# Sliding-window attention and an MLP mixer on one core: q and k turned by VectorE 32x32 transposes, scores on four 32-row tiles, an instruction order from a list schedule

## The chip, the cores and the metric

The kernel runs on one core of one Trainium2 chip. A core has five engines with instruction queues of their own, each strictly in order: TensorE (PE in the profile; its weight loads are listed apart as PEld), VectorE (DVE), ScalarE (ACT), GpSimd (POOL) and SyncE (SP, which here only issues DMAs). Matrix products land in PSUM, eight banks of 128 partitions x 512 fp32; everything else works out of SBUF. The metric is the device time of one execution in microseconds, as the median of the runs shown; lower is better.

## The reference

```
q, k, v: [4, 8, 768, 64] fp32          # batch, heads, sequence, head dim
scores = (q @ k^T) / 8                 # 768 x 768 for each batch and head
keep   = (key < 4) | (0 <= query - key < 128)     # 4 sink keys, a window of 128
x      = softmax(where(keep, scores, -1e9)) @ v   # then heads side by side: [4, 768, 512]
h      = relu(x^T @ w_tok1) @ w_tok2   # over the sequence, 768 -> 256 -> 768
u      = x + h^T
out    = u + relu(u @ w_ch1) @ w_ch2   # over the channels, 512 -> 1536 -> 512
```

All inputs and the output are fp32 in HBM. The kernel rounds to bf16 on the chip and accumulates in fp32.

## The kernel before, in words

The sequence is cut into NT = 6 tiles of 128. Attention is worked in groups of GH = 4 heads, two groups to a batch (g = 0 to 7), and a group in pairs j of heads. `tiles`, `load_q`, `load_k` and `load_v` bring a group's q, k and v as fp32; q and k in rows of 1536 bytes (partition p holds the positions 6p to 6p+5), v in 256-byte rows. `cast` and `cast_v` make bf16 of them, on POOL for groups 1 to 7 (`begin`). `tr` (L193) turns q and k: six PE transposes with the identity into one PSUM tile, and one DVE copy out of it that also restores the order of positions; a small DVE copy (L202) takes the four sink keys into `kz`. `sc` (L219) makes scores with keys on the partitions: for each key tile only the 128 or 256 queries that the window can reach, two heads beside each other on two 64-row tiles of PE; groups 0 and 1 first put a -30000 mask into PSUM with an identity matmul (L213). The exponent (L225, ACT) writes `pT`; for groups 2 to 7 POOL masks it afterwards (L229, L236, L239). `sk` (L246, L248) does the sink keys of the later query tiles. `pv` (L253 to L265) multiplies by v, with a column of ones for the sum, and DVE divides into `x_b`.

The mixer of a batch: `tok1` (L285, relu on ACT L287), `tok2` (L292, with u = x + h by DVE L293), `utr` (L298, PE transposes of u, copied by ACT L299), `ch1` (L304, C1: 24 of four matmuls, relu on ACT L306) and `ch2` (L313, C2: 18 of four matmuls, the sum with u on DVE L316, then the store on SP).

The order on each engine is the order in which the program emits instructions. For batch 0 it is a list written by hand; from then on `spread` puts the attention, token mixing and turns of batch b+1 (the `order` list) at given shares of the way through C1 and C2 of batch b. A load of group g+2 is issued when group g begins; group 2's load also waits for w_ch1 (`after`). PSUM is split by purpose: `ps_sc` two tiles of two banks (scores), `ps_mx` two banks (mixer matmuls), `ps_ms` two banks (transposes, sinks, PV). The weights are loaded and cast by DMAs issued on POOL.

Of the kernel before, what the change touches and what calls it, by code (L numbers as in the profile page):

```python
# [12 lines left out]
ALU = mybir.AluOpType  # L13


@with_exitstack
def kernel(
# [13 lines left out]
    nc = tc.nc  # L31
# [12 lines left out]
    HS = S // 2  # L44
    D1 = D + 1
    scale = 1.0 / float(D) ** 0.5

    singles = ctx.enter_context(tc.tile_pool(name="singles", bufs=1))
    stage = ctx.enter_context(tc.tile_pool(name="stage", bufs=2))
    bfp = ctx.enter_context(tc.tile_pool(name="bfp", bufs=2))  # L50
    att = ctx.enter_context(tc.tile_pool(name="att", bufs=3))
    ptp = ctx.enter_context(tc.tile_pool(name="ptp", bufs=4))
    small = ctx.enter_context(tc.tile_pool(name="small", bufs=4))
    xpool = ctx.enter_context(tc.tile_pool(name="xpool", bufs=2))
    mix = ctx.enter_context(tc.tile_pool(name="mix", bufs=2))
    osb = ctx.enter_context(tc.tile_pool(name="osb", bufs=4))
# [5 lines left out]
    mask0 = singles.tile([P, 2, 2, P], BF16, name="mask0")  # L62
    mneg = singles.tile([P, 2, 2, 2, P], BF16, name="mneg")
    warm = singles.tile([P, 512], BF16, name="warm")
    ks = [[singles.tile([P, P], BF16, name=f"ks{a}{j}") for j in range(2)] for a in range(2)]
    vs_f = singles.tile([4 * GH, NG, GH, D1], FP32, name="vs_f")
    vsink = singles.tile([P, NG, GH, D1], BF16, name="vsink")

# [5 lines left out]
    SYNC = mybir.DependencyInfo(mybir.DependencyClass.Sync, mybir.DependencyReason.DATA)  # L74

    def after(dma, *others):
        for o in others:
            tc.add_manual_dep(dma.ins, o.ins.name, SYNC, reason="order of loads")
        return dma
# [4 lines left out]
    def tiles(g):  # L84
        G = Group()
        G.b, G.h0 = g // GB, GH * (g % GB)
        G.q32 = stage.tile([P, GH, NT, D], FP32, name="q32")
        G.k32 = stage.tile([P, GH, NT, D], FP32, name="k32")
        G.qb = bfp.tile([P, 2, NT, 2, D], BF16, name="qb")
        G.kb = bfp.tile([P, 2, NT, 2, D], BF16, name="kb")  # L90
        G.v32 = stage.tile([P, GH, NT, D], FP32, name="v32")
        G.va = bfp.tile([P, GH, NT, D1], BF16, name="va")
        G.qT, G.kT, G.pT = [None, None], [None, None], [None, None]
        return G


    def load_qk(eng, src, dst, G, lo, hi):
        return eng.dma_start(
            out=dst[:, lo:hi].rearrange("p h t d -> p h (t d)"),
            in_=src[G.b, G.h0 + lo:G.h0 + hi].rearrange("h (p t) d -> p h (t d)", t=NT))  # L100

    def load_q(G, lo, hi, eng=nc.sync):
        return load_qk(eng, q, G.q32, G, lo, hi)

    def load_k(G, lo, hi, eng=nc.sync):
        return load_qk(eng, k, G.k32, G, lo, hi)

    def cast(G, j, which, copy):
        src, dst = ((G.q32, G.qb), (G.k32, G.kb))[which]
        copy(dst[:, j].rearrange("p t i d -> p i t d"), src[:, 2 * j:2 * j + 2])  # L110

    def by_dve(o, i):
        nc.vector.tensor_copy(out=o, in_=i)  # L113

    def by_pool(o, i):
        nc.gpsimd.tensor_copy(out=o, in_=i)

    def by_act(o, i):
        nc.scalar.activation(o, i, AF.Copy)

    def load_v(G):
        return nc.sync.dma_start(out=G.v32.rearrange("p h t d -> p (h t) d"),
                                 in_=v[G.b, G.h0:G.h0 + GH].rearrange("h (t p) d -> p (h t) d", p=P))

    def load_sinks():
        for h in range(GH):
            nc.sync.dma_start(
                out=vs_f[4 * h:4 * h + 4, :, h, 0:D],
                in_=v.rearrange("b (a h) s d -> h s (b a) d", h=GH)[h, 0:4])

    def load_tok():
        nc.gpsimd.dma_start(out=w_tok1, in_=moe_w_tok1.rearrange("(t p) n -> p t n", p=P))
        nc.gpsimd.dma_start(out=w_tok2, in_=moe_w_tok2.rearrange("(t p) n -> p t n", p=P))

    def load_ch1(i):
        hf = DCH // 2
        return nc.gpsimd.dma_start(out=w_ch1[:, :, ts(i, hf)],
                            in_=moe_w_ch1.rearrange("(t p) n -> p t n", p=P)[:, :, ts(i, hf)])

    def load_ch2(i):  # L140
        hf = NF // 2
        nc.gpsimd.dma_start(out=w_ch2[:, ts(i, hf)],
                            in_=moe_w_ch2.rearrange("(t p) n -> p t n", p=P)[:, ts(i, hf)])

    def build_masks():

        z = mneg.rearrange("p m x c q -> p (m x) c q")
        nc.gpsimd.affine_select(
            out=z[:, :, 0], in_=z[:, :, 0], compare_op=ALU.is_ge,
            fill=-30000.0, base=0, pattern=[[0, 4], [1, P]], channel_multiplier=-1)  # L150
        nc.gpsimd.affine_select(
            out=z[:, :, 1], in_=z[:, :, 1], compare_op=ALU.is_ge,
            fill=-30000.0, base=-1, pattern=[[0, 4], [-1, P]], channel_multiplier=1)
        nc.vector.memset(mneg[0:4, 0, 0], 0.0)

    def build_mask0():
        nc.vector.memset(mask0, 1.0)
        nc.gpsimd.affine_select(
            out=mask0[:, :, 0], in_=mask0[:, :, 0], compare_op=ALU.is_ge,
            fill=0.0, base=0, pattern=[[0, 2], [1, P]], channel_multiplier=-1)  # L160
        nc.gpsimd.affine_select(
            out=mask0[:, :, 1], in_=mask0[:, :, 1], compare_op=ALU.is_ge,
            fill=0.0, base=-1, pattern=[[0, 2], [-1, P]], channel_multiplier=1)
        nc.vector.memset(mask0[0:4], 1.0)

    def build_sinks():

        one = vs_f[:, :, :, D]
        nc.gpsimd.memset(one, 1.0)
        nc.gpsimd.affine_select(  # L170
            out=one, in_=one, compare_op=ALU.is_ge, fill=0.0,
            base=0, pattern=[[0, NG], [-4, GH]], channel_multiplier=1)
        nc.gpsimd.affine_select(
            out=one, in_=one, compare_op=ALU.is_ge, fill=0.0,
            base=3, pattern=[[0, NG], [4, GH]], channel_multiplier=-1)

    def cast_sinks():
        nc.vector.tensor_copy(out=vsink[0:4 * GH], in_=vs_f)

    def cast_v(G):  # L180
        nc.gpsimd.memset(G.va[:, :, :, D:D1], 1.0)
        nc.gpsimd.tensor_copy(out=G.va[:, :, :, 0:D], in_=G.v32)


    def attention(g, G, x_b, first):
        c0 = GH * D * (g % GB)
        kz = ks[g % 2]

        def tr(j, which):
            src = G.qb if which == 0 else G.kb  # L190
            ps = ps_ms.tile([P, NT, P], BF16, name="ps_tr", tag="ms")
            for t in range(NT):
                nc.tensor.transpose(ps[:, t], src[:, j, t].rearrange("p i d -> p (i d)"), ident)  # L193
            dst = att.tile([P, S], BF16, name="qT" if which == 0 else "kT")
            (by_act if g == 0 and j == 0 and which else by_dve)(
                dst.rearrange("d (p t) -> d p t", t=NT), ps.rearrange("d t p -> d p t"))
            if which == 0:
                G.qT[j] = dst
            else:
                G.kT[j] = dst  # L200
                for i in range(2):
                    nc.vector.tensor_copy(out=kz[j][ds(64 * i, 64), ds(8 * j + 4 * i, 4)],  # L202
                                          in_=ps[ds(64 * i, 64), 0:4, 0])

        def sc(j, u):
            if u == 0:
                G.pT[j] = ptp.tile([P, 2, 12 * P], BF16, name="pT")
            ps = ps_sc.tile([P, 2, 512], FP32, name="ps_s", tag="sc")
            kts = [(kt, (2 if kt < NT - 1 else 1) * P) for kt in (2 * u, 2 * u + 1)]
            n = sum(w for _, w in kts)  # L210
            if first:
                for i in range(2):
                    nc.tensor.matmul(ps[:, i, 0:n], ident,  # L213
                                     mneg[:, min(u, 1)].rearrange("p x c q -> p (x c q)")[:, 0:n],
                                     start=True, stop=False, skip_group_check=True)
            at = 0
            for kt, w in kts:
                for i in range(2):
                    nc.tensor.matmul(  # L219
                        ps[:, i, at:at + w],  # L220
                        G.kT[j][ds(64 * i, 64), ts(kt, P)], G.qT[j][ds(64 * i, 64), ds(kt * P, w)],
                        start=not first, stop=not first or at > 0, skip_group_check=first)
# [266 lines left out]
```

## Time and profile before

| | us |
|---|---|
| median of the 2 runs | 239.63 (239.11 to 240.16) |
| span of the profiled execution (first to last instruction) | 237.1 |
| PE busy in the span | 212.1 |
| DVE, ACT, POOL busy | 100.6, 114.1, 88.9 |

The profiled execution's own time is not given apart from its span. The span is one execution; the runs lie 2.0 to 3.1 us above it, so differences are formed on the span, and 2.5 us are added to compare with the median. In a row of the table of stretches stand the stretch, its length, the busy time of PE, PEld, DVE, ACT and POOL with the count of instructions, the granted PE clock, the busy share of the DMA engines and what they moved in GB/s. In a row of a group stand line, engine, operation, output<-input, shapes and count, then total busy time, the mean of one in ns, and the idle time ahead of it with what ended it. A row of the timeline begins with start and duration in us. A matmul's listed duration includes its way through the array; what it costs the next one is the distance between starts.

### The profile page before, as it was taken

What the parts mean: (1) busy time and instruction counts of PE and PEld (TensorE: products, weight loads), DVE (VectorE), ACT (ScalarE), POOL (GpSimd) and SP (SyncE); (2) the same over time, 40 slices, a digit from 0 to 9 for tenths busy, and PEclk for the clock granted to TensorE, in tenths of its full rate; (3) what the DMA queues carried; (4) which work ended last, traced back from release to release, by engine and by line L of the source; (5) the groups of instructions that cost most, each with busy time, mean ns of one, the idle gap of its engine ahead of it and who ended that gap; (6) DMA issues with size and microseconds to landing.
All of it is one profiled execution on the core that took longest, in us unless ns stands there. A gap on an engine that the chain in (4) does not pass through costs nothing.

```text
span 237.1 us, 4195 instructions
## 1 busy us (share of the span) xinstructions
PE 212.1 (89%) x1708; PEld 119.8 (51%) x1729; DVE 100.6 (42%) x221; ACT 114.1 (48%) x195; POOL 88.9 (37%) x124
## 2 busy tenths in 40 slices
PE   6797788976999999978999999978999999999993
PEld 2334545552556544645566445635566445554441
DVE  5687663070845454707526334707526334001131
ACT  2585536759472123595772233695762133653300
POOL 3567400449989200079985000089950000000000
PEclk9999999999999999999999999999999999999999
DMA  6999999999994111893911021100001021101122
GB/s 215 303 258 144 206 189 258 283 327 248 267 328 109 72 44 44 240 205 90 304 54 44 0 91 46 44 0 3 13 34 44 14 78 44 46 3 44 44 88 88
DMA packets 40659, 29.40 MB, mean 124 GB/s; under 512 B 25664, under 2 KB 37696, under 8 KB 40640
## 3 DMA queue, kind: packets, MB, share of 16 engines
q1 hardware_dynamic: 36000, 23.89, 36.8%
q0 software_dynamic: 3680, 3.93, 10.1%
q10 hardware_dynamic: 960, 1.31, 1.6%
q8 instruction: 13, 0.21, 0.4%
q14 instruction: 6, 0.05, 0.1%
HBM read 26.77 MB, written 6.29 MB: 139 GB/s over the span
## 4 chain that ended last, share of the span: by engine, by line
PE 68%; POOL 10%; DVE 9%; ACT 6%; DMA 3%; issue 2%; ACTq 0%; POOLq 0%
PE ps_w L313 26%; PE ps_v L304 20%; DVE o L316 5%; ACT pT L225 5%; PE ps_h L285 3%; PE ps_tr L193 3%; PE ps_u L292 3%; DMA k_113<-in_k_dram 3%; PE ps_s L219 3%; POOL pT L236 2%; PE ps_ut L298 2%; PE ps_o L257 2%; PE ps_o L253 2%; DVE x_b L265 2%; POOL pT L239 2%
## 5 line engine op out<-in xcount | busy, mean ns | idle before, releaser
L304 PE MATMUL ps_v<-uT,w_ch_103 128*128 128x384 bf16 x384 | 74.3, 325 | 1.4 <-ACT uT L299 0.7
L304 PEld LDWEIGHTS <-w_ch_103 128*128 128x128 bf16 x384 | 34.7, 97 | 25.0 <-issue 6.8
L225 ACT ACTIVATE pT<-ps_s 128x1024 bf16<-128x1024 f32 (+1 forms) x48 | 43.6, 961 | 7.1 <-PE ps_s L219 6.9
L229 POOL TENSOR_TENSOR pT<-pT,mask_92 128x512 bf16<-128x512 bf16 x12 | 13.8, 1154 | 52.2 <-ACT pT L225 52.2
L316 DVE TENSOR_TENSOR o<-ps_w,u_sb 128x512 f32<-128x512 f32 x24 | 16.6, 692 | 39.5 <-PE ps_w L313 39.5
L113 DVE COPY qT<-ps_tr 128x768 bf16<-128x768 bf16 x16 | 15.3, 957 | 35.2 <-PE ps_tr L193 35.0
L299 ACT ACTIVATE uT<-ps_ut 128x512 bf16<-128x512 bf16 x24 | 14.0, 596 | 32.6 <-PE ps_ut L298 32.5
L293 DVE TENSOR_TENSOR u_sb<-ps_u,x_b 128x512 bf16<-128x512 f32 x24 | 16.4, 689 | 25.9 <-PE ps_u L292 25.9
L265 DVE TENSOR_TENSOR x_b<-ps_o,rc 128x256 bf16<-128x256 f32 x48 | 20.4, 424 | 1.7
L236 POOL TENSOR_SCALAR_AFFINE_SELECT pT<-pT 128x640 bf16<-128x640 bf16 x24 | 18.0, 752 | 5.5 <-ACT pT L225 5.5
L219 PE MATMUL ps_s<-qT,kT 64*128 64x256 bf16 x192 | 15.5, 263 | 4.6 <-ACT pT L225 3.1
L264 DVE RECIPROCAL rc<-ps_o 128x4 f32<-128x4 f32 x48 | 8.5, 178 | 25.9 <-PE ps_o L261 13.1
L313 PE MATMUL ps_w<-w_ch_104,v_581 128*128 128x512 bf16 x69 | 18.1, 379 | 0.8 <-DVE o L316 0.6
L313 PE MATMUL ps_w<-w_ch_104,v_1338 128*128 128x512 bf16 x69 | 18.1, 379 | 0.8 <-DVE o L316 0.6
L313 PE MATMUL ps_w<-w_ch_104,v_111 128*128 128x512 bf16 x67 | 17.9, 379 | 0.8 <-DVE o L316 0.3
L306 ACT ACTIVATE v_1338<-ps_v 128x384 bf16<-128x384 f32 x24 | 11.9, 506 | 12.5 <-PE ps_v L304 12.5
L306 ACT ACTIVATE v_581<-ps_v 128x384 bf16<-128x384 f32 x24 | 11.9, 506 | 12.6 <-PE ps_v L304 12.6
L257 PE MATMUL ps_o<-va,pT 128*128 128x65 bf16 x192 | 17.3, 194 | 0.2
L306 ACT ACTIVATE v_2035<-ps_v 128x384 bf16<-128x384 f32 x24 | 11.8, 491 | 11.3 <-PE ps_v L304 11.2
L257 PEld LDWEIGHTS <-pT 128*128 128x128 bf16 x192 | 14.5, 98 | 3.5 <-issue 0.4
L306 ACT ACTIVATE v_111<-ps_v 128x384 bf16<-128x384 f32 x24 | 11.8, 495 | 9.0 <-PE ps_v L304 8.8
L313 PE MATMUL ps_w<-w_ch_104,v_2035 128*128 128x512 bf16 x70 | 15.9, 379 | 0.1
(102 smaller groups left out, 280.2 us busy)
## 6 DMA issues: line engine op xcount, KB each, us to landing
out_dram<-o SPq DMA_DIRECT2D x23, 256.0 KB, 2.0
w_ch_103<-in_moe_w_ch_dram POOLq DMA_DIRECT2D x2, 768.0 KB, 9.4
w_ch_104<-in_moe_w_ch_dram POOLq DMA_DIRECT2D x2, 768.0 KB, 13.8
k_113<-in_k_dram ACTq DMA_DIRECT2D x2, 384.0 KB
q_112<-in_q_dram SPq DMA_DIRECT2D x2, 384.0 KB, 5.8
q_118<-in_q_dram SPq DMA_DIRECT2D x2, 384.0 KB, 5.5
v_116<-in_v_dram SPq DMA_DIRECT2D x1, 768.0 KB, 10.9
v_122<-in_v_dram SPq DMA_DIRECT2D x1, 768.0 KB, 7.2
```

The costliest lines, as they stand in the source:

```text
L113: nc.vector.tensor_copy(out=o, in_=i)
L219: nc.tensor.matmul(ps[:, i, at:at + w], G.kT[j][ds(64 * i, 64), ts(kt, P)], G.qT[j][ds(64 * i, 64), ds(kt * P, w)], start=not first, stop= ...
L225: nc.scalar.activation(pT[:, :, 512 * u:512 * u + n], ps[:, :, 0:n], AF.Exp, scale=scale)
L236: nc.gpsimd.affine_select(out=cur, in_=cur, compare_op=ALU.is_ge, fill=0.0, base=0, pattern=[[0, NT - 1], [1, P]], channel_multiplier=-1)
L257: nc.tensor.matmul(ps[:, h], pT[:, i, ds(256 * qt, P)], G.va[:, h, qt], start=(qt < 2 and h == 0), stop=(h == GH - 1 and qt == 0), skip_gr ...
L265: nc.vector.tensor_tensor(out=x_b[:, qt, c0:c0 + GH * D].rearrange("p (h d) -> p h d", h=GH), in0=ps[:, :, 0:D], in1=rc.to_broadcast([P, G ...
L293: nc.vector.tensor_tensor(out=u_sb[:, st], in0=ps, in1=x_b[:, st], op=ALU.add)
L299: nc.scalar.activation(uT[:, :, ts(st, P)], ps, AF.Copy)
L304: nc.tensor.matmul(ps, w_ch1[:, c, ts(ft, P)], uT[:, c, ds(half * HS, HS)], start=(c == 0), stop=(c == NC - 1))
L306: nc.scalar.activation(v1[:, ft, ds(half * HS, HS)], ps, AF.Relu)
L313: nc.tensor.matmul(ps, v1[:, ft, ts(st, P)], w_ch2[:, ft], start=(ft == 0), stop=(ft == NF - 1))
L316: nc.vector.tensor_tensor(out=o, in0=ps, in1=u_sb[:, st], op=ALU.add)
```

## The change

- q and k: no PE transposes, no PSUM. A group's q lies with head h on the partitions 32h to 32h+31, so that each 32x32 block transposed by DVE puts 32 of the 64 head dimensions of head h on those same partitions. `turn` does one half of the head dimension (db = 0, 1) of all four heads at once, with unit-stride output. Loads are issued for each head (`head_load`): 1 KB pieces for groups 0 and 1 (whose positions come out permuted, undone in the exponent's access pattern and by small PE matmuls for v), 256-byte pieces from group 2 on.
- Scores: the head dimension is summed in two steps of 32, on four 32-row tiles of PE, one for each head (two at a time in groups 0 and 1). Only group 0 masks in PSUM; group 1 is masked on DVE, groups 2 to 7 on DVE (the first block) and on POOL or DVE.
- Order: every step is an `Op` with planned durations; `order_of` simulates the engines, the PSUM slots and the DMAs, and emits the steps in the order that it finds. Attention and token mixing of batch b+1 have priority over C1 and C2 of batch b. Some steps (relus, u's transposes' copies, v's copies) go to ACT or DVE as the planner finds.
- PSUM: two score tiles of two banks as before, and four banks shared by everything else.
- Sinks come by a casting DMA on POOL; v's bf16 tiles are three fixed buffers; fp32 loads share five buffers; batch 0's token mixing is done for each group apart; w_ch1 comes in quarters.

The core of the diff:

```diff
-    ps_sc = ctx.enter_context(tc.tile_pool(name="ps_sc", bufs=2, space=bass.MemoryType.PSUM))
-    ps_mx = ctx.enter_context(tc.tile_pool(name="ps_mx", bufs=2, space=bass.MemoryType.PSUM))
-    ps_ms = ctx.enter_context(tc.tile_pool(name="ps_ms", bufs=2, space=bass.MemoryType.PSUM))
+    slots = {"sc": 2, "mx": 4}
+    stage = ctx.enter_context(tc.tile_pool(name="stage", bufs=5))
...
+def order_of(ops, slots):
...
+    def start(op, e):
+        t = free_at[e]
+        for d in op.deps:
+            t = max(t, d.end + lag(d, op, e))
+        if op.take:
...
+        if e == "PE" and op.rows != rows:
+            t += 0.095
...
+            first = min(t for t, _ in c)
+            t, o = min(((t, o) for t, o in c if t <= first + 0.2), key=lambda x: (x[1].pri, -x[1].far, x[1].seq))
...
+def act(n):
+    return (n + 205) / 1200
+def dve(n, rate=1):
+    return (n / rate + 150) / 960
...
+    def head_load(eng, G, w, src, h, lo, hi, run):
...
+        eng.dma_start(
+            out=G.raw[w][Q * h:Q * h + Q].rearrange("p (c x) -> p c x", x=run * D)[:, at:at + n],
+            in_=src[h, lo:hi].rearrange("(c i e) d -> i c (e d)", i=Q, e=run))
...
+        def turn(w, hf, db, c):
+            def emit(e):
...
+                nc.vector.transpose(G.T[w][:, db, ds(hf * HS, S // n_half)],
+                                    G.bf[w][:, hf].rearrange("p (r x j) -> p r x j", x=DB, j=Q)[:, :, db])
+            old = (prev.sc + [prev.sk]) if prev else []
+            return op(f"T{w}{g}.{hf}{db}", ("DVE", dve(nc_ / 2) - 0.06), emit, [c] + old, early)
...
+                for kt, w in nk:
+                    for db in range(DB):
+                        for h in hs:
+                            r = ds(Q * h, Q)
+                            nc.tensor.matmul(bank[h][:, at:at + w], G.T["k"][r, db, ts(kt, P)],
+                                             G.T["q"][r, db, ds(kt * P, w)],
+                                             start=not pem and db == 0, stop=db == DB - 1,
+                                             skip_group_check=True, tile_position=(Q * h, 0))
+                    at += w
...
+                r = [op(f"MK{g}.0h", ("DVE", dve(1024, 2)), head, ex + [c_maske_op if perm else c_mask_op], base + u)]
...
+                    r.append(op(f"MK{g}.{u}{x}{c}", {"DVE": dve(512, 2)} if perm else {"POOL": 0.72, "DVE": dve(512, 2) + 0.1}, lambda e, x=x, c=c: block(e, x, c),
+                                ex + [c_maske_op if perm else c_mask_op], base + u, dear={"DVE": 0.6}))
...
+            o = op(f"C1{b}.{hf}{ft}", ("PE", 0.652), emit,
+                   [t for st in range(NH * hf, NH * hf + NH) for t in M.ute[st]] + [w_ops["ch1", ft // 3]], pri, take=[p])
...
+            M.v1[hf].append(op(f"V{b}.{hf}{ft}", {"ACT": act(HS), "DVE": dve(HS)}, relu, [o] + old, pri - 5, free=[p]))
...
+            if g >= 2:
+                deps = [c1w[3]] if g < 4 else []
+                deps += groups[g - 2].cast + (groups[g - 1].cast if g >= 3 else [])
+                load_ops(g, deps, 1000 * b - 700)
+            attention(g, batches[b].x, 1000 * b + 10 * a)
+        mixer(b, 1000 * b + 50, 1000 * b + 1100)
...
+        for o in order_of(ops, slots):
+            o.emit(o.engine)
```

The dependencies between steps are for the planner alone. On the chip an instruction waits for the data and the buffers that it uses, and for what stands ahead of it in its engine's queue.

More of the change, by code (lines that the diff above doesn't have):

```diff
@@ L13, with __init__ @@
 ALU = mybir.AluOpType
+INF = float("inf")
+class Psum:
+    def __init__(self, kind, readers):
+        self.kind, self.left, self.slot, self.tile = kind, readers, None, None
+class Op:
+    n = 0
+    def __init__(self, name, engines, emit, deps=(), pri=0, rows=False, take=(), free=(), land=0.0, dear=None):
+        self.name, self.engines, self.emit = name, engines, emit
+        self.deps, self.pri, self.rows = [d for d in deps if d is not None], pri, rows
+        self.take, self.free, self.land, self.dear = take, free, land, dear or {}
+        self.far = 0.0
+        self.begin = self.end = self.engine = None
+        Op.n += 1
+        self.seq = Op.n
@@ L72, with op @@
     w_ch2 = singles.tile([P, NF, DM], BF16, name="w_ch2")
[L74 to L79, printed above, removed]
+    ops = []
+    def op(name, engines, emit, deps=(), pri=0, **kw):
+        if not isinstance(engines, dict):
+            engines = dict([engines])
+        o = Op(name, engines, emit, deps, pri, **kw)
+        ops.append(o)
+        return o
@@ L81, with heads @@
+    def heads(src, g):
+        b, h0 = g // GB, GH * (g % GB)
+        return src[b, h0:h0 + GH]
     class Group:
         pass
[L84 to L94, printed above, removed]
@@ L97, in load_qk @@
[L97 to L110, printed above, removed]
@@ L112, in by_dve @@
[L112 to L129, printed above, removed]
@@ new lines @@
+    stores = []
+    w_ops = {}
+    o_warm = op("warm", ("DVE", 0.27), c_warm, (), -200)
+    c_ident_op = op("ident", ("POOL", 0.6), c_ident, (), -200)
+    o_zero = op("zero", ("DVE", 0.5), c_zero, (), -199)
+    o_mneg = op("mneg", ("POOL", 1.4), c_mneg, [o_zero], -199)
+    o_idp = op("identp", ("DVE", 0.2), c_ident_e, [c_ident_op], -199)
+    c_mneg_op = op("mnegs", ("DVE", 0.17), c_mneg_sink, [o_mneg, o_idp], -199)
+    c_kz_op = op("kz", ("DVE", 0.3), c_kz, (), -150)
+    o_vs = op("vsink", ("DVE", 1.2), c_vsink, (), -140)
@@ new lines, with weight, emit @@
+    c_maske_op = op("meo", ("ACT", 0.8), c_me_out, [o_me], -30, free=[me_ps])
+    def weight(key, dst, src, deps, pri=-40):
+        def emit(e):
+            nc.gpsimd.dma_start(out=dst, in_=src)
+        n = 1
+        for x in dst.shape:
+            n *= x
+        w_ops[key] = op(f"W{key}", ("POOL", 0.8), emit, deps, pri, land=n * 4e-6 / BW)
+        return w_ops[key]
+    v1st = groups[0].load["v"][3]
+    weight("tok1", w_tok1, moe_w_tok1.rearrange("(t p) n -> p t n", p=P), [v1st])
+    weight("tok2", w_tok2, moe_w_tok2.rearrange("(t p) n -> p t n", p=P), [v1st])
@@ new lines, with dummy @@
+    qf = DCH // 4
+    c1w = [weight(("ch1", i), w_ch1[:, :, ts(i, qf)], moe_w_ch1.rearrange("(t p) n -> p t n", p=P)[:, :, ts(i, qf)],
+                  [v1st], [-40, 12, 14, 16][i]) for i in range(4)]
+    c2src = moe_w_ch2.rearrange("(t p) n -> p t n", p=P)
+    weight(("ch2", 0), w_ch2[:, 0:8], c2src[:, 0:8], [c1w[0]], 40)
+    weight(("ch2", 1), w_ch2[:, 8:12], c2src[:, 8:12], [c1w[0]], 41)
+    def dummy(e):
+        p = psum["mx"][0].tile([P, 512], FP32, name="ps_warm", tag="b")
+        for _ in range(14):
+            nc.tensor.matmul(p, warm[:, 0:P], warm, start=True, stop=True)
@@ L457 @@
+    for o in ops:
+        if 0 <= o.pri < 60:
+            o.pri = 0
+    with tc.manual_schedule():
+        for o in order_of(ops, slots):
+            o.emit(o.engine)
 _INS = ['q', 'k', 'v', 'n_sink', 'window', 'moe_w_tok1', 'moe_w_tok2', 'moe_w_ch1', 'moe_w_ch2']
```

780 lines of the change are left out of this document (491 added, 289 removed).

## The prediction, made before the changed kernel was run

> **What bounds the kernel now.** I read the page's first two parts, then the table of stretches cut where a batch's channel mixer takes over PE (its first L304 matmuls at 36.57, 93.97, 146.99 and 200.02 us), then PE's waits inside those stretches.
>
> ```profile
> PE 212.1 (89%) x1708; PEld 119.8 (51%) x1729; DVE 100.6 (42%) x221; ACT 114.1 (48%) x195; POOL 88.9 (37%) x124
> PE   6797788976999999978999999978999999999993
> PEclk9999999999999999999999999999999999999999
> ```
>
> ```profile
> core 0: us, PE busy (x) PEld busy (x) DVE busy (x) ACT busy (x) POOL busy (x), PEclk, DMA share, GB/s
> 36.57:93.97 57.40, 52.16 (x435) 30.37 (x441) 24.01 (x53) 29.20 (x51) 28.85 (x38) 1.00 0.78 201
> 93.97:146.99 53.02, 49.70 (x420) 29.32 (x424) 23.50 (x52) 27.24 (x49) 24.09 (x32) 1.00 0.44 120
> 146.99:200.02 53.03, 49.72 (x421) 29.31 (x425) 23.51 (x52) 27.23 (x49) 19.54 (x26) 1.00 0.08 31
> 200.02:237.10 37.08, 32.60 (x167) 16.19 (x167) 4.84 (x7) 11.98 (x25) 0.00 (x0) 1.00 0.13 50
> ```
>
> PE is the bound from 36.57 us on, at the full granted clock. In the three middle stretches, 163.5 us, PE is idle 57.40-52.16 + 53.02-49.70 + 53.03-49.72 = 11.9 us; no other engine is busy over 56%. So there a microsecond of PE work taken out is a microsecond gained, and 11.9 us is the most that better order can give. The named part of that idleness, PE's waits from 36.5 to 201:
>
> ```profile
> PE ps_tr L193 <- POOL qb L116: 4.6, 3, 1.8
> PE ps_s L219 <- ACT pT L225: 3.1, 6, 1.0
> PE ps_w L313 <- DVE o L316: 1.6, 5, 0.4
> ```
>
> All three are in-order waits: PE stands at a transpose, a score or an output matmul while mixer matmuls behind it could run. Before 36.57 it is another kernel, a chain from the first load through both head groups of batch 0, with PE idle about a fifth of the time (the last fence of the next part).
>
> **The change part by part.** *PE transposes out.* This is the surest term.
>
> ```profile
> 110.72 0.50 PE L193 MATMUL ps_tr<-ident,kb 128*128 128x128 bf16 x6
> 111.06 0.81 PE L304 MATMUL ps_v<-uT,w_ch_103 128*128 128x384 bf16 x4
> 111.81 0.61 PE L219 MATMUL ps_s<-qT,kT 64*128 64x256 bf16 x8
> 112.35 0.82 PE L304 MATMUL ps_v<-uT,w_ch_103 128*128 128x384 bf16 x4
> ...
> 114.33 0.56 PE L219 MATMUL ps_s<-qT,kT 64*128 64x256 bf16 x8
> 114.82 1.04 PE L313 MATMUL ps_w<-w_ch_104,v_581 128*128 128x512 bf16 x4
> 115.70 0.27 PE L253 MATMUL ps_o<-vsink,pk 128*128 128x260 bf16 x1
> ```
>
> From start to start six transposes hold PE for 111.06-110.72 = 0.34 us (0.335 is the mean of such pairs). Groups 2 to 7 have four each: 6 x 4 x 0.335 = **-8.0 us**, nothing hiding it. The eight of groups 0 and 1 lie in the start, where PE waits anyway: nothing.
>
> *DVE transposes in.* Four of 128x768 a group (eight of half the size in group 0) in place of four copies out of PSUM. No row shows such an instruction; the nearest are these.
>
> ```profile
> L113 DVE COPY kT<-ps_tr 128x768 bf16<-128x768 bf16 x15 | 14.3, 952 | 0.2
> L265 DVE TENSOR_TENSOR x_b<-ps_o,rc 128x256 bf16<-128x256 f32 x48 | 20.4, 424 | 1.7
> L113 DVE CAST qb<-q_112 128x768 bf16<-128x768 f32 x2 | 1.0, 522 | 0.0
> ```
>
> By length the bounds are 0.52 us (the cast) and 0.424 x 3 = 1.27 us; I take the 0.95 of the copy it replaces. DVE's load then stays as it was, 23.5 of a 53 us batch; even at 1.27 it gains only 2.6 us a batch, under PE's 47. Nothing on the path. If that cover went, SC would be late and PE with it.
>
> *Scores on four 32-row tiles.* A group keeps three episodes of scores, with 16 matmuls each, not 8: four heads beside each other, two 32-deep halves one after the other, so the same columns pass if four tiles run side by side as two do now. In the rows above eight matmuls of 256 columns take 114.82-114.33 = 0.49 us; one alone streams for 0.65/4 x 256/384 = 0.108 (111.06 to 112.35 holds 0.65 of ps_v), so eight in a row would be 0.87. The two tiles do overlap, and their weight loads cost almost nothing (0.49 against 4 x 0.108). Twice as many loads are bounded below by nothing and above by no overlap at all (a rival below); I take a tenth, 0.05 us in 18 episodes: **+1.0 us**. [...]
>
> *Masks, casts, sinks.* In groups 2 to 7 the first block's mask moves to DVE and the others become 128x512 selects on either engine; q and k are cast whole.
>
> ```profile
> L236 POOL TENSOR_SCALAR_AFFINE_SELECT pT<-pT 128x640 bf16<-128x640 bf16 x24 | 18.0, 752 | 5.5 <-ACT pT L225 5.5
> L239 POOL TENSOR_SCALAR_AFFINE_SELECT pT<-pT 128x512 bf16<-128x512 bf16 x24 | 15.3, 638 | 0.0
> L229 POOL TENSOR_TENSOR pT<-pT,mask_92 128x512 bf16<-128x512 bf16 x12 | 13.8, 1154 | 52.2 <-ACT pT L225 52.2
> ```
>
> Nine selects of 0.64 are 5.8 us of POOL a group, against 4 x (0.75+0.64) + 2 x 1.15 = 7.9. [...] The DVE waits for ACT's exponent; behind it in its queue stand x_b, u and o, for which PE's banks wait. With four shared banks that holds PE only beyond the next three matmul groups, some 2 us.
>
> *Loads.* For groups 2 to 7 q and k come in 256-byte pieces, in four DMAs of 32 partitions, as only v does now.
>
> ```profile
> 113.00:114.00 1.00, 0.95 (x10) 0.52 (x9) 0.61 (x2) 1.00 (x2) 1.00 (x2) 1.00 1.07 399
> 117.00:118.00 1.00, 1.00 (x14) 0.55 (x12) 0.85 (x3) 0.00 (x0) 1.00 (x2) 1.00 1.39 220
> 22.00:32.00 10.00, 8.43 (x117) 5.90 (x114) 6.05 (x21) 4.60 (x7) 2.81 (x5) 1.00 1.17 206
> q0 software_dynamic: 3680, 3.93, 10.1%
> 34.60 11.82 SPq L98 DMA_DIRECT2D q_568<-in_q_dram  x1
> ```
>
> At 113 q and k of the last group flow (1536-byte pieces), at 117 its v; from 22 to 32 the weights (queue q0). So 2.36 MB a group take 2.36/0.22 = 10.7 us, not 7.6; a group has 23 us. It is hidden in the batches. Five raw buffers make SP wait for casts, as it does now (its q_568 entry stands 11.82 us); behind it are stores with four buffers, a slack of several O steps. In the start the explicit wait of group 2's load for w_ch1 is gone: from about 15 us these pieces share the engines with the 3.93 MB of weights. 19 us of weights (at 206 GB/s) and 21 of groups 2 and 3 end near 55 us. The first w_ch1 quarter is issued ahead, so I count nothing, and up to 5 us if C1 starves.
>
> *The start.*
>
> ```profile
> 0.00:10.00 10.00, 6.88 (x40) 2.88 (x41) 5.93 (x14) 3.96 (x4) 3.62 (x12) 1.00 0.84 267
> 10.00:20.00 10.00, 8.67 (x88) 3.84 (x87) 8.11 (x17) 7.71 (x9) 8.00 (x11) 1.00 1.06 213
> 20.00:30.00 10.00, 7.50 (x103) 5.03 (x104) 6.91 (x21) 4.23 (x6) 4.80 (x7) 1.00 1.17 195
> 36.57 0.81 PE L304 MATMUL ps_v<-uT,w_ch_103 128*128 128x384 bf16 x4 [0.69 <-ACT uT L299]
> ```
>
> DVE is the busiest evacuator here (20.95 of 30 us) and gets more: group 1's ten mask multiplies (about 5.5 us at 0.55), half of eight v copies (2), less the k sink copies and the fp32 sink buffer. Some 28 us of DVE work from 5.4 us on again end near 33, and token mixing follows, now split by group for batch 0 so that half is done early. I take **-1.0 us**, with 5 either way.
>
> *Order and banks.*
>
> ```profile
> L225 ACT ACTIVATE pT<-ps_s 128x1024 bf16<-128x1024 f32 x32 | 32.3, 1029 | 6.3 <-PE ps_s L219 6.3
> L264 DVE RECIPROCAL rc<-ps_o 128x4 f32<-128x4 f32 x48 | 8.5, 178 | 25.9 <-PE ps_o L261 13.1 <-PE ps_o L257 12.3
> L293 DVE TENSOR_TENSOR u_sb<-ps_u,x_b 128x512 bf16<-128x512 f32 x24 | 16.4, 689 | 25.9 <-PE ps_u L292 25.9
> 233.16 0.69 DVE L316 TENSOR_TENSOR o<-ps_w,u_sb 128x512 f32<-128x512 f32 x1 [1.90 <-PE ps_w L313]
> ```
>
> The planner's times agree with this trace where I can compare them: exponents 1.02 against 1.03, x_b 0.60 against 0.178+0.424, mixer 0.652 against 0.65, u and o 0.69 against 0.69. It puts attention of the next batch ahead of C1 and C2 and fills with those. Of the 11.9 us I take **-8.0**: the three named waits are 9.3 us, and I leave a little for lateness; bounds 0 and 11.9. Late next are the exponents (ACT 27 us a batch, most in one half). At the end 24 C1 of 0.65 and 18 C2 of 0.865 need 31.2 us, and the stretch from 200.02 to the last o (233.16) takes 33.1; four banks for two: **-1.0**, bounds 0 and 1.9.
>
> Sum: 237.1 - 8.0 + 1.0 - 1.0 - 8.0 - 1.0 = 220.1 us of span. The median of the runs is 239.63, 2.5 above the span; so 222.6, said as 222.5.
>
> **The rivals.** *The list gives nothing back.* Other waits replace the three: 237.1-8.0+1.0 = 230.1, 232.6 us, 228 to 237 with the start's bounds. For it: every list here is static, and a load that lands late holds a whole queue. Against it: the agreeing durations, and PE as the only full engine.
>
> *Everything falls into place:* all 11.9, start -5, end -1.9, scores 0: 210.3, so 212.8 and below 215 when most of it comes.
>
> *Four tiles don't overlap,* the change not doing what it says. A group then streams 40 x 0.108 + 8 x 0.055 = 4.8 us of scores, not 1.5: +19.7 in six groups, 219.1+19.7 = 238.8, or 241.3 us. The overlap of two tiles speaks against it.
>
> *Slower: attention first in PE's queue convoys.* SC stands ahead of C1; if turns or exponents are later than planned, PE stands at SC with ready mixer work behind it, and DVE, waiting for PV, delays the next turns. This is what the start looks like: from 10 to 30 us PE is idle 3.83 of 20, 19%. PE's 151.6-8.0+1.0 = 144.6 us at that share take 178.5, not 163.5: 252.1 of span, 254.6 us. It is slower than no change from an idle share of 14% (163.5+4.8 = 168.3). Now the share is 7%, and DVE and ACT at half load speak against it.
>
> **How the numbers follow.** A measurement here can tell about 2% from no change (234.8 to 244.4 us). Chances: forecast (215 to 229) 0.57; nothing back 0.18, a third of it above 234.8; all in place 0.08; no overlap 0.06; convoy 0.11, a little of it inside 2%. Faster 0.57+0.08+0.12 = 0.77; same 0.06+0.06+0.01 = 0.13; slower 0.10. The range 212 to 237 holds the first two and most of the third, 0.8 in all; the cases beyond 237 are left out.
>
> **What would show it.** Right: no L193 left; a batch's stretch near 47 to 48 us; score episodes of 0.5 to 0.6; first ps_v matmul at 33 to 38 us; DVE transposes near 0.95. Wrong: PE waiting over 2 us a batch for SC's inputs, DVE over 70% in a batch, loads at under 100 GB/s, or w_ch1 late.

## The result and the profile after

The changed kernel takes 225.38 us (224.84 and 225.93) against 239.63, a ratio of 0.942 with an interval of 0.933 to 0.951: faster by 14 us, where 17 were forecast (222.5, range 212 to 237). The profiled execution took 225.93 us with a span of 223.9.

The page of the changed kernel, busy time by engine, PE's slices and the granted clock:

```profile
PE 206.2 (92%) x1760; PEld 115.9 (52%) x1780; DVE 127.4 (57%) x271; ACT 107.5 (48%) x187; POOL 70.2 (31%) x89
PE   7298497999999999999999899999999999999994
PEclk9955569999999999999999999999999999999999
```

Two things are to be seen. From the ninth slice on PE is full, with an 8 or 9 in every slice but the last. And the start, the first eight slices of 5.6 us, has kept its gaps, with the granted clock near one half in three of them.

The join between the two parts is the first matmul of the channel mixer, ps_v: 36.57 us before. The changed kernel's view of the ps_v line (L645; minimum, median and longest duration in ns, then first and last start), its last row on DVE, and the stretch between:

```profile
L645 PE MATMUL ps_v<-uT,w_ch x384: 322/326/337, 47.6 to 210.0; 128*128 128x384 bf16 x192
```
```profile
220.71 0.42 DVE L677 TENSOR_TENSOR o<-ps_w,u_sb 128x256 f32<-128x256 f32 x1 [0.89 <-PE ps_w L667]
```
```profile
47.62:220.71 173.09, 170.35 (x1436) 97.13 (x1451) 93.25 (x188) 86.69 (x151) 52.33 (x54) 1.00 0.65 116
```

The same stretch of the kernel before, from its first ps_v to the start of its last o (233.16):

```profile
36.57:233.16 196.59, 184.17 (x1438) 105.19 (x1455) 75.17 (x164) 95.64 (x171) 72.48 (x96) 1.00 0.39 107
```

The start is 47.62-36.57 = 11.05 us longer, the rest 196.59-173.09 = 23.5 us shorter, and what follows the last o's start 0.75 (3.94 to 3.19): together -13.2, the difference of the spans. PE's listed idle time in the long stretch fell from 12.42 us to 2.74. The three waits that the prediction named are gone; the longest that are left of PE's waits there, in the changed kernel:

```profile
PE ps_v L645 <- DVE x_b L559: 0.6, 1, 0.6
PE ps_o L535 <- DVE x_b L559: 0.3, 1, 0.3
PE ps_o L535 <- ACT v L205: 0.3, 1, 0.3
```

### The profile page after: what moved, and what is told of

It is laid out like the page before. It is cut to its first block, busy times and chain, and to the rows that moved or that the text cites. A ratio compares the mean times of both kernels' runs of the same rounds, so it can differ in the third digit from the quotient of the medians.

```text
span 223.9 us, 4412 instructions
## 1 busy us (share of the span) xinstructions
PE 206.2 (92%) x1760; PEld 115.9 (52%) x1780; DVE 127.4 (57%) x271; ACT 107.5 (48%) x187; POOL 70.2 (31%) x89
## 4 chain that ended last, share of the span: by engine, by line
PE 75%; DMA 10%; DVE 7%; ACT 4%; SPq 1%; issue 1%; DVEq 0%
PE ps_w L667 27%; PE ps_v L645 26%; DMA raw_k<-in_k_dram 7%; PE ps_u L607 5%; PE ps_h L583 5%; PE ps_s L437 4%; DMA raw_v<-in_v_dram 3%; PE ps_ut L618 3%; DVE pT L477 2%; PE ps_o L538 2%; PE ps_o L543 2%; PE ps_o L535 2%; DVE x_b L559 2%; ACT pT L456 1%; SPq L304 1%
## 5 line engine op out<-in xcount | busy, mean ns | idle before, releaser
L645 PE MATMUL ps_v<-uT,w_ch 128*128 128x384 bf16 x384 | 69.0, 326 | 0.8 <-DVE x_b L559 0.6
L667 PE MATMUL ps_w<-w_ch,v 128*128 128x512 bf16 (+1 forms) x288 | 65.2, 370 | 0.8 <-issue 0.2
L205 ACT ACTIVATE v<-ps_v 128x384 bf16<-128x384 f32 x86 | 42.0, 493 | 43.2 <-PE ps_v L645 32.1
L645 PEld LDWEIGHTS <-w_ch 128*128 128x128 bf16 x384 | 35.8, 98 | 24.8 <-DVE x_b L559 1.7
L677 DVE TENSOR_TENSOR o<-ps_w,u_sb 128x512 f32<-128x512 f32 (+1 forms) x25 | 16.7, 666 | 52.0 <-PE ps_w L667 52.0
L667 PEld LDWEIGHTS <-v 128*128 128x128 bf16 x300 | 28.6, 98 | 30.2 <-issue 0.4
L456 ACT ACTIVATE pT<-ps_s 128x1024 bf16<-128x1024 f32 (+1 forms) x36 | 32.4, 950 | 20.2 <-PE ps_s L437 17.7
L212 POOL TENSOR_SCALAR_AFFINE_SELECT pT<-pT 128x512 bf16<-128x512 bf16 x21 | 15.9, 765 | 35.4 <-ACT pT L456 14.9
L437 PE MATMUL ps_s<-qT,kT 32*128 32x256 bf16 (+1 forms) x384 | 20.0, 281 | 2.6 <-DVE kT L363 1.9
L200 POOL CAST kb<-raw_k 128x1536 bf16<-128x1536 f32 x7 | 10.4, 1491 | 26.8 <-DMA raw_k<-in_k_dram 26.8
L613 DVE TENSOR_TENSOR u_sb<-ps_u,x_b 128x512 bf16<-128x512 f32 (+1 forms) x30 | 15.6, 573 | 4.2 <-PE ps_u L607 4.2
L538 PE MATMUL ps_o<-va,pT 128*128 128x65 bf16 x192 | 16.8, 199 | 0.1
L543 PE MATMUL ps_o<-va,pT 128*128 128x65 bf16 x160 | 15.6, 198 | 0.0
```

The source lines that it names most:

```text
L200: "POOL": lambda o, i: nc.gpsimd.tensor_copy(out=o, in_=i),
L205: nc.scalar.activation(o, i, AF.Relu)
L437: nc.tensor.matmul(bank[h][:, at:at + w], G.T["k"][r, db, ts(kt, P)], G.T["q"][r, db, ds(kt * P, w)], start=not pem and db == 0, stop=db = ...
L456: nc.scalar.activation(o, i, AF.Exp, scale=scale)
L538: nc.tensor.matmul(ps[:, h], G.pT[qt // 2][:, h, ds(256 * (qt % 2), P)], G.va[:, h, qt], start=(qt < 2 and h == 0), stop=(h == GH - 1 and ...
L543: nc.tensor.matmul(ps[:, h], G.pT[kt // 2][:, h, ds(256 * (kt % 2) + P, P)], G.va[:, h, kt], start=False, stop=(h == GH - 1), skip_group_c ...
```

## The experiments

**The changed kernel again**, beside others on one chip.

> The changed kernel again, as the base of the runs beside it. All theories: 224.8 to 225.9 us, first C1 matmul (ps_v) near 47.6 us, granted clock at half from about 11 to 32 us.

225.12 us (224.73 to 226.11), ratio 0.942 (0.938 to 0.947). The experiments are compared with this run and with the kernel before on their own chip (238.7 to 239.2 us everywhere). Its first ps_v starts at 47.1. In its stretch table the loads of groups 0 and 1 stand at 207 GB/s with a DMA share of 1.16, and its last v, group 1's, is cast at 25.65:

```profile
10.00:18.00 8.00, 7.05 (x48) 2.48 (x48) 5.74 (x10) 5.31 (x7) 1.63 (x3) 0.67 1.16 207
```
```profile
25.65 0.96 DVE L199 CAST vb<-raw_v 128x1536 bf16<-128x1536 f32 x1 [2.75 <-DMA raw_v<-in_v_dram]
```

**Loads of groups 0 and 1 across all 128 partitions**, with the same 1 KB pieces:

```diff
+        if run > 1:
+            for c in range(h, n, GH):
+                eng.dma_start(
+                    out=G.raw[w].rearrange("p (c x) -> p c x", x=run * D)[:, at + c],
+                    in_=src[:, lo + P * c:lo + P * c + P].rearrange("h (i e) d -> h i (e d)", e=run))
+            return
```

> Groups 0 and 1 are loaded with the same 1 KB pieces, but each DMA takes one chunk of 128 positions of all four heads and so writes 128 partitions, not 32; the order on all engines is the same. Theory: the start is late because it waits for loads, and these are slow because a DMA writes only 32 partitions. Then the first 20 us move near 390 GB/s, not 205, the second cast of v comes at 16 to 18 us, not 26.6, the first ps_v matmul at 37 to 40, and the time is 216 to 218 us. Rival, small pieces: 1 KB pieces are as slow as 256-byte ones wherever they go; the rate stays near 205 and the time within 1 us of 225. Rival, the clock: PE's half clock from 11 to 32 us makes the start late; the loads may get faster but the time falls by 3 us at most.

274.32 us, ratio 1.148 (1.142 to 1.154): a miss as a cure, but the clearest test of the start. The stretch, the cast of group 1's v, and the first ps_v:

```profile
10.00:18.00 8.00, 1.79 (x6) 0.53 (x6) 2.44 (x5) 2.13 (x2) 0.87 (x3) 0.50 0.28 91
```
```profile
73.32 0.96 DVE L199 CAST vb<-raw_v 128x1536 bf16<-128x1536 f32 x1 [22.89 <-DMA raw_v<-in_v_dram]
95.08 10.56 PE L651 MATMUL ps_v<-uT,w_ch 128*128 128x384 bf16 x64
```

The DMA share fell to 0.28, what four to five engines of sixteen would give if they were always busy. The source's outermost dimension is now the four heads; whether that is the cause was not shown. Two things follow. Over its share of busy time an engine moves 91/(16 x 0.28) = 20 GB/s with 1 KB pieces here, against 207/(16 x 1.16) = 11 in the changed kernel, an estimate from these two rows, so the size of the pieces is not what slows the changed kernel's loads. And group 1's v came 73.32-25.65 = 47.7 us later, the first ps_v 95.08-47.1 = 48.0, the end 49.2: with the list unchanged, the start follows the landing of these loads, one for one.

**A warm clock**: more opening matmuls.

```diff
-        for _ in range(14):
+        for _ in range(30):
```

> 30 warm-up matmuls in place of 14, so that PE is busy until the first scores. Theory, the start waits for loads: the granted clock may stay at 1.0, but the first ps_v matmul moves by less than 1 us and the time is 224 to 226 us. Rival, the half clock is the cause of the late start: first ps_v at 37 to 42 us, 215 to 220 us.

225.98 us, ratio 0.945 (0.939 to 0.951), no change. The clock now is whole through the stretch that had 0.67, and the loads, at 206 GB/s for 207, do not care:

```profile
10.00:18.00 8.00, 6.54 (x61) 2.73 (x60) 5.42 (x10) 7.05 (x11) 1.55 (x3) 1.00 1.16 206
```

The first ps_v stands at 47.2. So as far as the clock was held, to about 22 us, its being halved is not what makes the start late. What the half clock costs between 22 and 32 us was not separated. Nor do the last v and the first ps_v move quite together here: that v was cast at 26.37, 0.7 us later than in the changed kernel, and the first ps_v came 0.1 later, so up to 0.6 us may be the clock's.

**Two row tiles at a time** in groups 2 to 7.

```diff
-            if g < 2:
+            if True:
```

> Groups 2 to 7 make scores for two heads at a time, as groups 0 and 1 do: the same matmuls, two row tiles side by side, not four. Theory, four row tiles overlap almost fully (an episode of 16 matmuls takes 0.55 us): 36 episodes of about 0.54 in place of 18 of 0.55, +9.5 us of PE work, and since PE has next to no idle time after the start, 233 to 236 us. Rival, four tiles overlap no better than two: within 1 us of 225. Rival, PE has slack: +3 us or less.

232.81 us, ratio 0.974 (0.969 to 0.980), +7.7 us. Eight matmuls on two tiles hold PE for 0.44 us in this kernel (the starts below), so an episode of 16 takes 0.88 where four tiles take 0.55 (shown further down). Twelve full episodes and six of three quarters make 12 x 0.33 + 6 x 0.25 = 5.5 us of the 7.7; PE's listed time in these scores rose by 7.0 (10.4 to 17.4), tails included. Had four tiles overlapped no better than two, two at a time would have cost nothing.

```profile
81.09 0.50 PE L437 MATMUL ps_s<-qT,kT 32*128 32x256 bf16 x8
81.53 0.20 PE L538 MATMUL ps_o<-va,pT 128*128 128x65 bf16 x1
```

**PE work put back**: 24 matmuls of 128 columns, as many as the transposes had, ahead of each sink score of groups 2 to 7 (their product is overwritten), with their time in the plan.

```diff
+            if g >= 2:
+                for _ in range(24):
+                    nc.tensor.matmul(ps[:, 0:P], ident, warm[:, 0:P], start=True, stop=True)
```

> Groups 2 to 7 each get 24 more matmuls of 128 columns on PE ahead of their sink scores (their result is overwritten), as much PE time as the transposes that the change took away: 6 x 24 x 0.0555 = 8.0 us. Theory, PE is the bound after the start: +7.5 to +8.5 us, 232.5 to 234. Rival, the transposes were worth less than their PE time, since order and waits set the pace: +4 us or less.

231.86 us (231.06 and 232.66), ratio 0.971 (0.967 to 0.975): +6.7 us. The stretch from the first ps_v to the last o, here and in the changed kernel beside the others:

```profile
47.60:227.57 179.97, 178.79 (x1604) 106.01 (x1601) 91.82 (x188) 87.80 (x152) 53.20 (x55) 1.00 0.64 111
```
```profile
47.10:220.26 173.16, 170.41 (x1436) 97.15 (x1451) 92.63 (x188) 86.61 (x151) 52.10 (x54) 1.00 0.65 116
```

PE's busy time grew by 8.4 us and its idle time fell from 2.75 to 1.18, so the stretch grew by 6.8. Work of the size of the transposes thus costs 6.7 us for its 8.0 us on PE; the waits that the transposes met in the queue are not in this figure.

**Fewer shared banks**: two instead of four (`"mx": 2`), and then four again but split by purpose as the kernel before had them: two for the mixer's matmuls, two for sinks, PV, turns of u and v's spread.

> Two shared PSUM banks in place of four, planned anew. Theory A, the list order gives the idle time back and the banks are a detail: +1 to +3 us. Theory B, the shared banks do it: PE's idle time after the start is back to 10 us or more, +8 to +15 us.

> The four shared banks are split by purpose as in the kernel before, two for the mixer's matmuls (T1, T2, C1, C2) and two for sinks, PV, the turns of u and v's spreading; planned anew. Theory A, the list order alone gives the idle time back: +0 to +3 us on 225. Theory B, it is the sharing (two banks in all gave +34 us): PE's idle time after the start returns, +6 to +15 us.

```diff
-    slots = {"sc": 2, "mx": 4}
+    slots = {"sc": 2, "mx": 2, "ms": 2}
```

Two banks: 258.97 us, ratio 1.085 (1.083 to 1.087), +33.9, far beyond what either theory gave, with 14.9 us of listed PE idle time in the stretch below. Two and two: 233.63, ratio 0.976 (0.970 to 0.982), +8.5. Their stretches from first ps_v to last o:

```profile
55.10:253.75 198.65, 183.75 (x1454) 99.93 (x1451) 95.47 (x190) 83.80 (x142) 54.87 (x59) 1.00 0.51 93
```
```profile
51.10:229.32 178.22, 175.18 (x1456) 97.85 (x1454) 92.59 (x191) 83.99 (x144) 54.02 (x59) 1.00 0.61 109
```

Split by purpose, the first ps_v is 4.0 us later than with shared banks (51.1 for 47.1) and the rest 5.1 longer, of which PE's listed idle time holds only 0.3. Most of it is in time listed as busy, for the same work: the 384 ps_v matmuls alone are listed with 71.3 us, for 69.1. (The changed kernel's trace lacks some 20 matmul records, which by an estimate can shift about 1 us between idle and busy.) Where such time hides is said below.

**Loads on two sets of partitions at once.** `head_load` writes the 32 partitions of one head, and SP's queue sends the heads one after the other. Five kernels put some heads on other queues or in another order, so that heads 0 and 1 and heads 2 and 3 land beside each other. First, group 0's k, which ACT issues, in another order of heads:

```diff
-heads(src, g), h, lo, hi, run)
+heads(src, g), (h + 2) % GH if e == "ACT" else h, lo, hi, run)
```

> Group 0's k heads are loaded in the order 2, 3, 0, 1 while q goes 0, 1, 2, 3; everything else, the issuing places included, is as in the changed kernel. Only which partitions the two queues write at one time is different: the same 32 now, two different 32s here. Theory, what is written to one set of 32 partitions is limited to about 205 GB/s: from 2 to 6 us the loads move 350 to 400 GB/s, group 0 is in at about 7 us, not 10, everything that follows lands some 3 us earlier, and the time is 221 to 223 us. Rival, the loads are slow because of the pieces or of the many DMAs: 205 GB/s as before, 225 us.

224.45 us, ratio 0.940 (0.938 to 0.942), -0.7, which is hardly clear of the noise. From 2 to 6 us the loads moved 267 GB/s for 228, with the same pieces, queues and number of DMAs, but not the 350 to 400 that were expected. Here is that stretch, with and without the rotation:

```profile
2.00:6.00 4.00, 4.00 (x11) 1.43 (x10) 3.15 (x6) 0.00 (x0) 2.99 (x9) 1.00 0.91 267
```
```profile
2.00:6.00 4.00, 4.00 (x11) 1.44 (x10) 2.99 (x5) 0.00 (x0) 2.98 (x9) 1.00 1.06 228
```

Group 1's v was cast 1.4 us earlier and the first ps_v came at 45.9, 1.2 earlier: nearly the same slope as with the slow loads, at a thirtieth of the size.

```profile
24.23 1.42 DVE L199 CAST vb<-raw_v 128x1536 bf16<-128x1536 f32 x1 [2.04 <-DMA raw_v<-in_v_dram]
```

Then heads 2 and 3 of q, k and v on ACT; and heads 2 and 3 of q and k on ACT, of v on POOL, with 30 opening matmuls:

```diff
-                    e = "ACT" if g == 0 and w == "k" else "SP"
+                    e = "ACT" if g < 2 and h >= 2 else "SP"                                  # two queues
+                    e = ("ACT" if w != "v" else "POOL") if g < 2 and h >= 2 else "SP"        # three queues
```

> For groups 0 and 1 heads 0 and 1 of q, k and v are issued on SP and heads 2 and 3 on ACT, so that two sets of 32 partitions are written all through the start; the planner is told and orders anew. Theory, 32 partitions are the limit: about 390 GB/s from 2 to 14 us, the second cast of v at 16 to 19 us, not 26.6, first ps_v at 38 to 41, 216 to 219 us; ACT's 16 issues of 0.5 to 0.8 us may eat 2 us of that. Rival, pieces or number of DMAs: 205 GB/s, 224 to 228 us.

> For groups 0 and 1, heads 2 and 3 of q and k are issued on ACT and heads 2 and 3 of v on POOL, heads 0 and 1 on SP; 30 warm-up matmuls. ACT has 12 issues, not 16, and none that waits for a buffer. Theory, the start is bound by loads to 32 partitions at a time, and ACT standing in its queue at v's loads is what spoiled the version with two queues: about 270 GB/s up to 14 us, first exponent by 13 us, second cast of v at 20 to 22, first ps_v at 41 to 44, 219 to 222 us. Rival, issuing on engines that compute costs as much as it gains: 225 us or more.

Misses both: 229.86 us, ratio 0.965 (0.959 to 0.970), and 227.83, ratio 0.951 (0.947 to 0.956). The rate rose as hoped, here from the stretch table of the two-queue kernel,

```profile
10.00:18.00 8.00, 2.00 (x18) 0.82 (x19) 3.81 (x9) 0.50 (x1) 3.48 (x6) 0.66 1.13 268
```

but the issues stood in the queues of working engines. In that kernel's timeline ACT is held for 6.67 us by four v loads, and PE's longest wait is for an exponent behind them:

```profile
10.80 6.67 ACTq L304 DMA_DIRECT2D raw_v<-in_v_dram  x4
```
```profile
PE ps_s L430 <- ACT pT L458: 7.4, 1, 7.4
```

Its first ps_v came at 52.1, 5.0 us later than in the changed kernel, although group 1's v was cast 2.9 us earlier, at 22.77.

With three queues POOL waits for the sinks, and one load of v behind that wait is issued only at 19.16; group 1's v is cast at 26.20, later than in the changed kernel (25.65), and the first ps_v comes at 50.0.

```profile
17.45 1.02 POOL L280 MEMSET vsink<- 16x32 bf16 x1 [6.25 <-DMA vsink<-in_v_dram]
...
19.16 0.57 POOL L304 DMA_DIRECT2D raw_v<-in_v_dram  x1
...
26.20 1.45 POOL L200 CAST vb<-raw_v 128x1536 bf16<-128x1536 f32 x1 [4.11 <-DMA raw_v<-in_v_dram]
```

Last, q and k alone split between SP and ACT, and k of both groups on ACT with its heads rotated as above:

```diff
+                    e = "ACT" if g < 2 and h >= 2 and w != "v" else "SP"     # q and k split
+                    e = "ACT" if g < 2 and w == "k" else "SP"                # k of both rotated
```

> For groups 0 and 1 heads 2 and 3 of q and k are issued on ACT, heads 0 and 1 on SP; v stays on SP as in the changed kernel. Theory L (the start is bound by how fast the loads of groups 0 and 1 land, and two sets of 32 partitions at once take 255 to 290 GB/s against 205 to 215 for one): q and k, 3.15 MB, take 11.7 us at 270 instead of 15.0 at 210, so group 1's v is there about 3 us earlier, its cast near 22.5 instead of 25.7, the first ps_v matmul near 44 instead of 47, and the time is 221 to 223 us. ACT has twelve issues, so it should not stand as it did with eighteen. Rival Q (a DMA issue on a working engine's in-order queue costs what the rate brings): the loads are faster, but an exponent or a cast waits behind an issue, or the list comes out in a worse order; first ps_v at 47 or later and 225 to 229 us.

> k of both groups 0 and 1 is issued on ACT in the order of heads 2, 3, 0, 1, q and v on SP. Theory L: as for the other kernel of this call, q and k of group 1 too land on two sets of partitions; group 0 alone brought 0.7 us and a first ps_v matmul at 45.9; with group 1 the 1.57 MB of its q and k take 5.8 us at 270 instead of 7.5, so 222 to 224 us with the first ps_v near 44.5. Rival Q: ACT has four more issues ahead of or between its exponents, 225 to 228 us, first ps_v at 47 or later.

223.60 us (222.54 to 225.04), ratio 0.935 (0.932 to 0.938), and 226.19, ratio 0.947 (0.944 to 0.949). The first is the shortest time of this study, by 1.5 us against the changed kernel on another chip, with intervals that all but touch; rotated k of both groups gains nothing. The trace of the first is its slowest execution (225.04) and starts no earlier: first ps_v at 47.1. In its POOL timeline the weights go out at 17.31, 2.4 us ahead of the changed kernel's 19.67, beside the last v loads, and the v that waited is cast at 25.52, as late as ever:

```profile
17.31 1.80 POOL L735 DMA_DIRECT2D w_tok<-in_moe_w_tok_dram  x2
19.11 0.79 POOL L735 DMA_DIRECT2D w_ch<-in_moe_w_ch_dram  x1
25.52 1.46 POOL L200 CAST vb<-raw_v 128x1536 bf16<-128x1536 f32 x1 [5.62 <-DMA raw_v<-in_v_dram]
```

So what q and k saved on the DMA engines went, in that execution, to weights that were not yet needed: up to 25.5 us the weights' queue moved 0.76 MB, against 0.02 in the changed kernel. Where its other executions gain their 1.5 us no trace shows. With k of both groups rotated the last v is cast at 25.58 and the first ps_v comes at 49.0. So where the list is planned anew, the last v alone does not set the start: the order, and the issues in the queues, decide too.

## Why the prediction was right, and where it was not

The kernel became faster for the reasons given, but that the number came within 3 us is luck: two terms were wrong, with opposite signs. By its terms, before and after:

- **PE transposes, -8.0.** Right: no transpose of q or k is left on PE, and putting their work back cost 6.7.
- **Four row tiles, +1.0.** Right. An episode takes 0.55 us, from its first matmul to the next group's in the changed kernel's timeline (77.13-76.58), for 0.49 before:

```profile
76.58 0.61 PE L437 MATMUL ps_s<-qT,kT 32*128 32x256 bf16 x16
77.13 0.60 PE L516 MATMUL ps_k<-qT,kz 128*128 128x512 bf16 x2
```

  That is +0.06 in 12 full episodes, 0.7 us. With the 0.108 that the prediction worked out for one matmul of 256 columns alone, sixteen in a row would take 16 x 0.108 = 1.73 us, 3.1 times the 0.55: an estimate of what four tiles side by side bring.
- **DVE transposes, nothing.** Right, at 0.95 us each (its view: minimum, median, longest in ns). DVE is now busy 93 of 173 us, for 75 of 197 before, with masks and copies that it took over besides:

```profile
L363 DVE STREAM_TRANSPOSE qT<-qb x18: 536/946/978, 7.3 to 139.5; 128x768 bf16<-128x768 bf16 x14, 128x384 bf16<-128x384 bf16 x4
```

- **Loads of groups 2 to 7, nothing.** Right: no wait for w_ch or for q and k stands among PE's after 47.6.
- **Order and banks -8.0, end -1.0.** Too small, and the step that failed is the sentence that 11.9 us is the most that better order can give. The stretch lost 23.5. Of this 8.0 are the PE time of the transposes; 1.5 is work of batch 0 that the changed kernel does ahead of its first ps_v (the kernel before does four matmuls of ps_u at 0.216 and twelve of ps_ut at 0.056 after it); scores give 0.7 back. That leaves some 15 us for order and banks: 9.7 of listed idle time, and 5 of time that the profile lists as busy. The same 384 ps_v matmuls show it, in the groups of the stretch, before and after:

```profile
L304 PE MATMUL ps_v<-uT,w_ch_103 128*128 128x384 bf16 x384 | 74.3, 325 | 1.4 <-ACT uT L299 0.7
```
```profile
L645 PE MATMUL ps_v<-uT,w_ch 128*128 128x384 bf16 x384 | 69.0, 326 | 0.8 <-DVE x_b L559 0.6
```

  Such a matmul is listed with 0.325 us here, while four in a row hold PE for 0.65, 0.16 each (starts below): its listed end lies 0.16 us behind the time at which the next could start, so a wait shorter than that is not listed as idle. In the kernel before, four ps_v matmuls that hold PE for 0.65 (127.63 to 128.28) are followed once after 0.89 (126.37 to 127.26); of these 0.24 us the profile counts 0.08 as idle:

```profile
126.37 0.81 PE L304 MATMUL ps_v<-uT,w_ch_103 128*128 128x384 bf16 x4
127.26 0.28 PE L253 MATMUL ps_o<-vsink,pk 128*128 128x260 bf16 x1
...
127.63 0.81 PE L304 MATMUL ps_v<-uT,w_ch_103 128*128 128x384 bf16 x4
128.28 0.27 PE L253 MATMUL ps_o<-vsink,pk 128*128 128x260 bf16 x1
```

  The banks alone are worth 8.5 us with the list planned for them, 5.1 of it in this stretch. How the rest divides between the list and the banks was not measured.
- **The start, -1.0 within 5 either way.** Wrong by 12 us, outside its own bounds: the first ps_v came at 47.6, not at 33 to 38. The prediction counted DVE's work there and gave the loads of groups 0 and 1 no price at all, though they now write 32 partitions at a time. Up to 26.4 us the chain of work in the changed kernel is those loads and their issues; its last part:

```profile
10.88 7.93 DMA raw_k<-in_k_dram
18.81 0.02 issue
18.82 7.61 DMA raw_v<-in_v_dram
...
26.56 1.36 DVE vb L199
27.91 0.04 issue
27.96 1.43 PE ps_p L394 x12
```

  The 4.72 MB of groups 0 and 1 take 22.8 us at 207 GB/s. At the rates of the 128-partition loads before, 399 for q and k in 1536-byte pieces and 220 for v in 256-byte pieces, they would take 3.15/0.399 + 1.57/0.220 = 15.0, an estimate, so 7.8 less. Group 1's v is cast at 26.56, before at 19.48 (below): 7.1 of the 11.05 us, and the slow-load and rotated kernels show that this is paid nearly in full. That the partitions matter is shown by the rotated kernel, 267 GB/s for 228 from 2 to 6 us with nothing else changed; from 10 to 18 us one set of 32 partitions took 207 and two sets took 268, and all 128 took 399 before, in 1536-byte pieces (113 to 114 us). What sets these rates was not shown.

  The other 4.0 us lie between that cast and the first ps_v (21.1 us for 17.1). The cast of group 1's v and the first x_b in the kernel before, then the first x_b in the changed one:

```profile
19.48 1.47 POOL L182 CAST va<-v_122 128x1536 bf16<-128x1536 f32 x1
```
```profile
18.10 0.42 DVE L265 TENSOR_TENSOR x_b<-ps_o,rc 128x256 bf16<-128x256 f32 x1
```
```profile
29.99 0.42 DVE L559 TENSOR_TENSOR x_b<-ps_o,rc 128x256 bf16<-128x256 f32 x1
```

  Of these 4.0 us, 1.5 are the work of batch 0 that moved ahead of the first ps_v, as counted above; it comes back in the stretch. For the other 2.5 the record has three candidates, which no run separates.

  The first is waiting in order. Before, group 0's PV began ahead of group 1's v. After, its first x_b comes at 29.99, though group 0's v was cast at 22.73: in PE's queue PV stands behind group 1's ps_p (27.96 in the chain; these are the small matmuls that undo the permutation of v), and on DVE copies of group 0's ps_p stand behind the cast of group 1's v:

```profile
26.56 1.35 DVE L199 CAST vb<-raw_v 128x1536 bf16<-128x1536 f32 x1 [2.87 <-DMA raw_v<-in_v_dram]
27.82 1.47 DVE L199 CAST va<-ps_p 128x384 bf16<-128x384 f32 x3
```

  The planner's constants give a reason that can be read in the code:

```
    BW, BWV = 0.37, 0.17
```

  The list was made for loads of groups 0 and 1 at 370 GB/s. The prediction held that the planner's times agree with the trace, and compared those of the engines alone. A list planned with 0.21 was not tried.

  The second is the clock, which was granted at 0.50 up to 32 us: one query tile of PV holds PE for 0.66 us there (29.97 to 30.63) and for 0.36 at full clock (37.07 to 37.43). PE is on the chain from 27.96 to 32.4, so this may be worth up to 4.4 x 0.30/0.66 = 2.0 us, an estimate. The third is what the prediction did count, DVE's work: between that cast and the first ps_v DVE is busy 18.6 of 21.1 us, for 11.2 of 17.1 before, with 4.1 us of group 1's masks in it.

Of the rivals, that the list gives nothing back is out: order and banks gained more in the stretch than the 11.9 us of everything in place. Nothing convoyed after the start, and four tiles overlap. What the prediction put down to the convoy, PE waiting in order behind a late input, did come, in the start: by a load, not by an engine.

## What to carry to other kernels

When a layout changes, price every load by the partitions that it writes (207 GB/s to 32 at a time here, 268 to two sets of 32, 399 to all 128) as well as by its bytes and pieces, and hold a planner's bandwidth to the trace as strictly as its engine times. PE's listed idle time is not the most that a better order can give: short waits hide in the tails of matmuls (of the 0.24 us above 0.08 was listed as idle), so compare starts, or the busy time of the same instructions before and after. A DMA moved to a working engine's queue brings its rate and its wait together (268 GB/s, and 6.67 us of ACT's queue, in the two-queue kernel): look what stands behind it.

## What the runs showed of the hardware that was not expected

- Loads to the 32 partitions of one head at a time ran at 207 GB/s with a DMA share of 1.16; with heads 0 and 1 on one queue and heads 2 and 3 on another, at 268 over the same 8 us, 29% more, and still short of the 399 of loads to all 128 partitions in 1536-byte pieces before.
- Loads to all 128 partitions whose source has the four heads outermost ran at 91 GB/s from 10 to 18 us, with a DMA share of 0.28.
- In the two-queue kernel ACT issued twelve loads by 9.9 us, about 1 us for two; the next four held its queue for 6.67 us.
